# Experts' second product: one weight load for both parts of the activations, two halves of a bank added per expert

## The chip, the cores and the metric

The kernel runs on one core of a Trainium2 chip. The metric is the device time of one execution in microseconds, the median of several runs. Engines are named as the profile names them: PE is TensorE's matmul, PEld its weight load, DVE is VectorE, ACT ScalarE, POOL GpSimd, SP SyncE, whose queue issues most DMAs.

## What is computed

The reference is a chain of three parts, all in fp32 (q, k, v of 2 batches x 8 heads x 768 x 64; 1536 tokens of 512 features; 8 experts):

```python
state = gamma * state + k_t (x) v_t;  y_t = scale * q_t @ state    # linear attention, per head
e = argmax(x @ w_gate);  disp[e, slot] = x                         # dispatch, 8 experts
h = np.maximum(np.einsum('ecd,edf->ecf', disp, w1), 0.0)           # 512 -> 1024
y = np.einsum('ecf,efd->ecd', h, w2)                               # 1024 -> 512
out[i] = gate_w[i] * y[expert_idx[i], pos[i]]
h = x @ w_in;  g = h / (1 + exp(-h));  out = g @ w_out             # 512 -> 2048 -> 512
```

The change touches the second product of the experts, `y`.

## The kernel before

**Precision.** PE multiplies in a format (`F32R`) with fewer bits than fp32. So every operand is kept as two tiles, a high part (the value rounded to that format) and a low part (the value minus the high part), and every product is three matmuls into one sum: high x high, high x low, low x high.

**The order of the work.** Attention with gate and routing fills the first 75 us. Then the eight experts follow, each with at most 216 tokens (`SL`) in columns. An expert has eight weight units of 128 x 1024 (512 KB each): four of the first product, `stage_a(e, fu)` (lines 847 to 867), and four of the second, `stage_b(e, fu)` (869 to 879). Each unit holds 8 blocks of 128 x 128 and takes 24 matmuls. After that `finish(e)` (881 to 888) moves the result out of PSUM, and at the end come 12 steps of the dense FFN over quarters `q` of its hidden layer and groups `g` of 512 tokens (`s1`, `s2`, lines 940 to 998).

**The order is written out by hand.** The pool runs in manual schedule: each engine executes its instructions in the order of the program. The loop at lines 1002 to 1025 is: gather the next expert's rows, four `stage_a`, four `stage_b` (after the second of them the transposes of the next expert's rows, `xprep`, lines 813 to 818 and 557 to 565), then `finish(e)`. For the last expert `finish(7)` comes after the first FFN step (1042).

**Feed.** `advance(u)` (823 to 835) stands at the head of each unit. It issues the split of unit `u + 3`: ScalarE writes the high part (line 164), VectorE the low part (168), and the low part is issued one piece late, so that `advance(u)` issues the high part of unit `u + 3` and the low part of unit `u + 2`. It also issues the DMAs of later units, whose buffers come free with that low part, and every sixth unit from unit 9 on it puts in one piece of the FFN's weights (`ffn_piece`, lines 172 to 205: four VectorE, three ScalarE and two GpSimd instructions). In experts 1 and 2 VectorE also computes the token masks (898 to 918), a part after each second `stage_b`.

**PSUM.** From the experts on all tiles come from one pool of eight banks of 512 fp32 columns (807 to 811). An expert takes four banks for `h`, two for `y` and two for the transposes.

`stage_a` ends with the Relu of `h`: high part by ScalarE (863), low part by VectorE (864), into two tiles `hhi` and `hlo`. `stage_b` calls `three` (839 to 845) for each block: 256 blocks in all, of 8 experts x 4 units x 2 (`f`) x 4 (`d`), and each call loads weights three times, twice the same ones. Two of the four output blocks `d` share a bank of `y`. `finish` then takes, per bank, one ScalarE copy of 432 columns into `x2hi` and one VectorE subtraction into `x2lo`, at a column offset held in a register.

Of the kernel before, what the change touches and what calls it, by code (L numbers as in the profile page):

```python
# [8 lines left out]
F32 = mybir.dt.float32  # L9
F32R = mybir.dt.float32r  # L10
# [5 lines left out]
ALU = mybir.AluOpType  # L16
# [6 lines left out]
E = 8  # L23
F1 = 1024
F2 = 2048
P = 128
# [3 lines left out]
KD = DM // P  # L30
# [10 lines left out]
GT = NTOK // NG  # L41
# [13 lines left out]
def slots(cap):  # L55

    cap = max(0, min(cap, NTOK))
    sl = min(SLOTS, max(1, -(-cap // P)) * P)
    return cap, -(-sl // P), sl, -(-max(0, cap - sl) // P)
# [33 lines left out]
def moe_chain_kernel(ctx: ExitStack, tc: tile.TileContext, cap: int, a, out: bass.AP):  # L93
    nc = tc.nc
    ctx.enter_context(tc.manual_schedule())

    cap, nmain, SL, nover = slots(cap)
# [3 lines left out]
    SP = nmain * P  # L101
# [452 lines left out]
    moe = moe_stack.enter_context(tc.tile_pool(name="moe", side="right", bufs=1, reuse_waits="tile"))  # L554
# [100 lines left out]
    x2hi = ffn.tile([P, KD, NTOK + SP], F32R, name="x2hi")  # L655
    x2lo = ffn.tile([P, KD, NTOK + SP], F32R, name="x2lo")
# [3 lines left out]
    def fetch(e):  # L660
        xrows[e] = [gather_rows(rows, e, j, "xr", toki) for j in range(nmain)]
# [14 lines left out]
    with tc.If(over > capm, label="over"):  # L676
        with tc.tile_pool(name="gen", side="right", bufs=1) as gen, tc.tile_pool(name="gps", side="right", bufs=2, space=PSUM) as gps:
# [12 lines left out]
                out=god[:, :E], in0=god[:, :E], scalar1=gov[:, E : E + 1], scalar2=float(-cap), op0=ALU.add, op1=ALU.add  # L690
# [17 lines left out]
            if nover > 0:  # L708
# [3 lines left out]
                for j in range(nover):  # L712
                    nc.vector.scalar_tensor_tensor(
                        out=gstf[:, j], in0=gov[:, :E], scalar=float(j * P), in1=gov[:, 1:], op0=ALU.add, op1=ALU.min
# [11 lines left out]
                    out=slot, in0=ecol, scalar1=float(nover * P), scalar2=float(-capm), op0=ALU.mult, op1=ALU.add  # L726
# [3 lines left out]
                    out=block, in0=slot, scalar1=0.5 - P / 2, scalar2=ROUND, op0=ALU.add, op1=ALU.add  # L730
# [7 lines left out]
                    out=gohb, in0=cst[:, C_W : C_W + E * nover].unsqueeze(1).to_broadcast([P, NT, E * nover]),  # L738
                    in1=block.unsqueeze(2).to_broadcast([P, NT, E * nover]), op=ALU.is_equal,
                )  # L740
                nc.vector.tensor_tensor(
                    out=gohb, in0=gohb, in1=tokv.unsqueeze(2).to_broadcast([P, NT, E * nover]), op=ALU.mult
# [3 lines left out]
                    out=gohp, in0=iota_p.unsqueeze(1).to_broadcast([P, NT, P]),  # L746
                    in1=slot.unsqueeze(2).to_broadcast([P, NT, P]), op=ALU.is_equal,
# [10 lines left out]
                with tc.For_i(0, E, 1) as e:  # L758
                    now = gen.tile([P, 2, nover], I32, name="now")
                    nc.vector.tensor_copy(  # L760
                        out=now.unsqueeze(1), in_=gall[:, bass.ds(e, 1)]
                    )
                    for j in range(nover):
# [9 lines left out]
                        for r in range(8):  # L773
# [3 lines left out]
                            if r < 4:  # L777
                                gwv = gw.rearrange("p (d f m) -> p d f m", d=KD, f=2)
                                for f in range(2):
                                    hp = gps.tile([P, P], F32, tag="hp", name=f"hp{j}_{r}_{f}")  # L780
                                    for d in range(KD):
                                        nc.tensor.matmul(
                                            hp, lhsT=gwv[:, d, f], rhs=gxt[:, d], start=d == 0, stop=d == KD - 1
                                        )
                                    nc.scalar.activation(gh[:, 2 * r + f], hp, AF.Relu)
                            else:
                                gwv = gw.rearrange("p (f d m) -> p f d m", f=2, d=KD)
                                for f in range(2):
                                    ff = 2 * (r - 4) + f
                                    for d in range(KD):  # L790
                                        nc.tensor.matmul(
                                            yp[:, d], lhsT=gwv[:, f, d], rhs=gh[:, ff],
                                            start=ff == 0 and d == 0, stop=ff == 7, skip_group_check=True,
                                        )

                        win = bass.ds(r0, P)
                        nc.scalar.copy(out=x2hi[:, :, win], in_=yp)
                        nc.vector.tensor_tensor(
                            out=x2lo[:, :, win], in0=yp, in1=x2hi[:, :, win].bitcast(F32), op=ALU.subtract
# [10 lines left out]
    def bank(name):  # L810
        return ps.tile([P, 512], F32, tag="ps", name=name)
# [25 lines left out]
    htiles = {}  # L837

    def three(out_ap, l, r, first, last):

        lh, ll = l
        rh, rl = r
        nc.tensor.matmul(out_ap, lhsT=lh, rhs=rh, start=first, stop=False, skip_group_check=True)  # L843
        nc.tensor.matmul(out_ap, lhsT=lh, rhs=rl, start=False, stop=False, skip_group_check=True)  # L844
        nc.tensor.matmul(out_ap, lhsT=ll, rhs=rh, start=False, stop=last, skip_group_check=True)  # L845

    def stage_a(e, fu):
        u = 8 * e + fu
        advance(u)
        whi, wlo = [t.rearrange("p (d f m) -> p d f m", d=KD, f=2) for t in unit_tiles.pop(u)]  # L850
        xhi, xlo = xts[e]
        skip = {"skip_group_check": True}
        hb = bank(f"h{e}_{fu}").rearrange("p (f t) -> p f t", f=2)[:, :, :SL]
        for f in range(2):
            for d in range(KD):
                nc.tensor.matmul(hb[:, f], lhsT=whi[:, d, f], rhs=xhi[:, d], start=f == 0 and d == 0, stop=False, **skip)  # L856
                nc.tensor.matmul(hb[:, f], lhsT=wlo[:, d, f], rhs=xhi[:, d], start=False, stop=False, **skip)  # L857
        for f in range(2):
            for d in range(KD):
                nc.tensor.matmul(hb[:, f], lhsT=whi[:, d, f], rhs=xlo[:, d], start=False, stop=d == KD - 1, **skip)  # L860
        hhi = moe.tile([P, 2, SP], F32R, tag=f"hhi{fu}", name=f"hhi{e}_{fu}")[:, :, :SL]
        hlo = moe.tile([P, 2, SP], F32R, tag=f"hlo{fu}", name=f"hlo{e}_{fu}")[:, :, :SL]
        nc.scalar.activation(hhi, hb, AF.Relu)
        nc.vector.scalar_tensor_tensor(
            out=hlo, in0=hb, scalar=0.0, in1=hhi.bitcast(F32), op0=ALU.max, op1=ALU.subtract
        )
        htiles[fu] = (hhi, hlo)

    def stage_b(e, fu, yb):
        u = 8 * e + 4 + fu  # L870
        advance(u)
        whi, wlo = [t.rearrange("p (f d m) -> p f d m", f=2, d=KD) for t in unit_tiles.pop(u)]
        hhi, hlo = htiles[fu]
        for f in range(2):
            for d in range(KD):
                three(
                    yb[d // 2][:, d % 2], (whi[:, f, d], wlo[:, f, d]), (hhi[:, f], hlo[:, f]),
                    fu == 0 and f == 0 and d % 2 == 0, fu == 3 and f == 1,
                )

    def finish(e, yb):
        win = bass.ds(offr[e], SL)
        for b in range(2):
            ds2 = slice(2 * b, 2 * b + 2)
            nc.scalar.copy(out=x2hi[:, ds2, win], in_=yb[b])
            nc.vector.tensor_tensor(
                out=x2lo[:, ds2, win], in0=yb[b], in1=x2hi[:, ds2, win].bitcast(F32), op=ALU.subtract
            )


# [111 lines left out]
    for e in range(E):  # L1002
        if e + 1 < E:
            fetch(e + 1)
        for fu in range(4):
            stage_a(e, fu)
            if e == 0 and fu == 1:
                places = Places(const, "moe", False, edge)
                nc.vector.tensor_copy(out=offi, in_=places.start)
        if e == 0:  # L1010
            offr = [place_reg(offi[0:1, j : j + 1], max(0, NTOK - SL * (E - j)), NTOK) for j in range(E)]
        if e == 1:
            chores = token_masks(places)
        if e == 3:
            run(chores)
            token_table()
        yb = [bank(f"y{e}_{j}").rearrange("p (d t) -> p d t", d=2)[:, :, :SL] for j in range(2)]
        for fu in range(4):
            stage_b(e, fu, yb)
            if fu % 2 == 0:  # L1020
                next(chores, None)
            if fu == 1 and e + 1 < E:
                xprep(e + 1)
        if e + 1 < E:
            finish(e, yb)
# [4 lines left out]
    f2 = ctx.enter_context(tc.tile_pool(name="f2", bufs=1, reuse_waits="tile"))  # L1030
# [79 lines left out]
```

## Time and profile before

| | us |
|---|---|
| median of 3 runs | 525.29 (524.22 to 527.42) |
| the profiled execution | 521.98 |
| its span, first to last instruction | 520.2 |
| PE busy | 506.1 (97%) |
| VectorE busy | 319.9 (61%) |
| ScalarE busy | 243.7 (47%) |
| GpSimd busy | 152.6 (29%) |

The span runs from the first to the last instruction; the execution's time holds 1.8 us more. Busy times are of one profiled execution. A matmul's recorded duration holds its latency: a new one starts long before the recorded end of the last, so PE's rhythm is read from the starts. Times in rows are in microseconds from the start of the span, unless marked ns.

### The profile page before, as it was taken

How to read it: one execution, taken by the hardware profiler on the slowest of the kernel's cores; microseconds unless marked ns; L12 is line 12 of the kernel's file. 1: busy time of each engine (PE TensorE's matmuls, PEld its weight loads, DVE VectorE, ACT ScalarE, POOL GpSimd, SP SyncE). 2: the span in 40 equal slices, each digit the busy share in tenths (PEclk: the TensorE clock that was granted, in tenths of full speed). 3: DMA queues.
4: the chain of work that ended last, by engine and by line, in shares of the span. 5: the costliest groups of instructions: out<-in, count | busy, mean ns of one | idle time of the engine just before them, and what ended most of it. 6: DMA issues, size and time to landing. Idle time of an engine off the chain costs nothing.

```text
span 520.2 us, 9255 instructions
## 1 busy us (share of the span) xinstructions
PE 506.1 (97%) x3590; PEld 454.1 (87%) x3590; DVE 319.9 (61%) x663; ACT 243.7 (47%) x404; POOL 152.6 (29%) x144
## 2 busy tenths in 40 slices
PE   7999699999999999999999999999999999999995
PEld 5989689999999999999988888888888888888885
DVE  2667756788987887686176756457466574232441
ACT  2345535566665566555255655554254542212110
POOL 2545530105313243021015333251132511000315
PEclk8999999999999999999999999999999999999998
DMA  8999845877686667862013222131121200000203
GB/s 283 320 333 315 330 129 199 306 259 252 231 286 215 238 238 247 260 225 83 1 40 121 83 81 82 40 122 40 42 81 42 82 1 0 0 1 0 82 20 141
DMA packets 27151, 76.11 MB, mean 146 GB/s; under 512 B 3553, under 2 KB 6497, under 8 KB 27106
## 3 DMA queue, kind: packets, MB, share of 16 engines
q1 hardware_dynamic: 24416, 67.53, 38.4%
q0 software_dynamic: 2256, 7.34, 3.9%
q8 instruction: 28, 0.46, 0.3%
q10 hardware_dynamic: 434, 0.64, 0.3%
q14 instruction: 17, 0.14, 0.1%
HBM read 69.20 MB, written 6.29 MB: 145 GB/s over the span
## 4 chain that ended last, share of the span: by engine, by line
PE 74%; issue 14%; DMA 5%; POOL 3%; DVE 2%; ACT 0%; POOLq 0%; SPq 0%; DVEq 0%; ACTq 0%
PE s L843 11%; PE s L844 11%; PE s L845 11%; PE h L856 6%; PE h L857 6%; PE y L843 6%; PE y L845 5%; PE y L844 5%; PE h L860 5%; DMA q<-q 4%; PE A L335 2%; POOL out L981 2%; PE y L368 1%; PE g L401 1%; DMA gq<-gq 1%
## 5 line engine op out<-in xcount | busy, mean ns | idle before, releaser
L199 POOL TENSOR_TENSOR w<-w,ex 128x512 f32<-128x512 f32 x32 | 41.4, 1293 | 223.9 <-DVE ex L196 212.7
L952 DVE TENSOR_TENSOR gv<-s,gv 128x512 f32<-128x512 f32 x48 | 33.2, 692 | 86.9 <-ACT gv L951 86.8
L168 DVE TENSOR_TENSOR lo<-raw,hi 128x1024 fp32r<-128x1024 f32 x62 | 82.0, 1336 | 3.2 <-issue 2.3
L843 PE MATMUL s<-x2hi,hi 128*128 128x512 f32 x192 | 74.7, 389 | 0.0
L845 PE MATMUL s<-x2hi,lo 128*128 128x512 f32 x192 | 74.7, 389 | 0.0
L844 PE MATMUL s<-x2lo,hi 128*128 128x512 f32 x192 | 74.7, 389 | 0.0
L951 ACT ACTIVATE gv<-s 128x512 f32<-128x512 f32 x48 | 28.8, 599 | 97.7 <-PE s L845 97.7
L843 PE MATMUL y<-hhi,hi 128*128 128x216 f32 x256 | 70.8, 277 | 0.0
L845 PE MATMUL y<-hhi,lo 128*128 128x216 f32 x256 | 70.2, 274 | 0.0
L844 PE MATMUL y<-hlo,hi 128*128 128x216 f32 x256 | 70.2, 274 | 0.0
L843 PE MATMUL s<-hi,ghi 128*128 128x512 f32 x176 | 68.5, 389 | 0.0
L844 PE MATMUL s<-lo,ghi 128*128 128x512 f32 x176 | 68.5, 389 | 0.0
L845 PE MATMUL s<-hi,glo 128*128 128x512 f32 x176 | 68.5, 389 | 0.0
L164 ACT CAST hi<-raw 128x1024 fp32r<-128x1024 f32 x64 | 65.6, 1048 | 4.5 <-issue 2.3
L856 PE MATMUL h<-xthi,hi 128*128 128x216 f32 x256 | 58.9, 274 | 0.3 <-ACT xthi L564 0.3
L857 PE MATMUL h<-xthi,lo 128*128 128x216 f32 x256 | 58.8, 274 | 0.0
L954 DVE TENSOR_TENSOR glo<-gv,ghi 128x512 fp32r<-128x512 f32 x48 | 36.3, 757 | 32.9 <-ACT ghi L953 32.9
L203 POOL TENSOR_TENSOR lo<-w,hi 128x512 fp32r<-128x512 f32 x32 | 47.4, 1482 | 22.4 <-ACT hi L202 22.4
L856 PEld LDWEIGHTS h<-xthi,hi 128*128 128x128 f32 x256 | 49.1, 192 | 0.4 <-ACT xthi L564 0.4
L845 PEld LDWEIGHTS y<-hhi,lo 128*128 128x128 f32 x256 | 49.2, 192 | 0.0
L844 PEld LDWEIGHTS y<-hlo,hi 128*128 128x128 f32 x256 | 49.1, 192 | 0.0
L857 PEld LDWEIGHTS h<-xthi,lo 128*128 128x128 f32 x256 | 49.1, 192 | 0.0
(140 smaller groups left out, 931.2 us busy)
## 6 DMA issues: line engine op xcount, KB each, us to landing
raw<-w SPq DMA_DIRECT2D x64, 512.0 KB, 4.4
raw<-w_in SPq DMA_DIRECT2D x16, 512.0 KB, 3.5
raw<-w_out SPq DMA_DIRECT2D x16, 512.0 KB, 3.3
vk<-vk SPq DMA_DIRECT2D x11, 512.0 KB, 6.6
q<-q SPq DMA_DIRECT2D x12, 256.0 KB, 5.6
xtok<-xr SPq DMA_DIRECT2D x12, 256.0 KB, 4.3
kt<-kt SPq DMA_DIRECT2D x11, 256.0 KB, 5.3
gq<-gq SPq DMA_DIRECT2D x10, 128.0 KB, 6.0
```

Of the source, the lines that this page charges most:

```text
L164: nc.scalar.copy(out=hi, in_=t)
L168: lo_eng.tensor_tensor(out=lo, in0=t, in1=hi.bitcast(F32), op=ALU.subtract)
L199: nc.gpsimd.tensor_tensor(out=w, in0=w, in1=ex.bitcast(F32), op=ALU.mult)
L203: nc.gpsimd.tensor_tensor(out=lo[:, sl], in0=w, in1=hi[:, sl].bitcast(F32), op=ALU.subtract)
L843: nc.tensor.matmul(out_ap, lhsT=lh, rhs=rh, start=first, stop=False, skip_group_check=True)
L844: nc.tensor.matmul(out_ap, lhsT=lh, rhs=rl, start=False, stop=False, skip_group_check=True)
L845: nc.tensor.matmul(out_ap, lhsT=ll, rhs=rh, start=False, stop=last, skip_group_check=True)
L856: nc.tensor.matmul(hb[:, f], lhsT=whi[:, d, f], rhs=xhi[:, d], start=f == 0 and d == 0, stop=False, **skip)
L857: nc.tensor.matmul(hb[:, f], lhsT=wlo[:, d, f], rhs=xhi[:, d], start=False, stop=False, **skip)
L951: nc.scalar.activation(gv, hb, AF.Sigmoid)
L952: nc.vector.tensor_tensor(out=gv, in0=hb, in1=gv, op=ALU.mult)
L954: nc.vector.tensor_tensor(out=glo, in0=gv, in1=ghi.bitcast(F32), op=ALU.subtract)
```

## The change

`hhi` and `hlo` become one tile `hh` with the two parts side by side. In `stage_b` the high part of the weights is loaded once per block, and one matmul passes both parts of the activations under it, 2 x 216 columns, into the two halves of a bank (columns 0 to 215 and 256 to 471). The low part of the weights then passes the high activations into the second half. Each output block `d` has its own bank, four per expert. `finish` copies the second half out (ScalarE), adds the first half to it (VectorE), casts the sum to the high part (ScalarE) and subtracts (VectorE), for each `d` by itself, over two small tiles `ys`; for the last expert these come from the FFN's pool, from the buffers of `gv`.

```diff
-        hhi = moe.tile([P, 2, SP], F32R, tag=f"hhi{fu}", name=f"hhi{e}_{fu}")[:, :, :SL]
-        hlo = moe.tile([P, 2, SP], F32R, tag=f"hlo{fu}", name=f"hlo{e}_{fu}")[:, :, :SL]
+        hh = moe.tile([P, 2, 2, SP], F32R, tag=f"hh{fu}", name=f"hh{e}_{fu}")[:, :, :, :SL]
+        hhi, hlo = hh[:, 0], hh[:, 1]
...
-        htiles[fu] = (hhi, hlo)
+        htiles[fu] = hh
...
-        hhi, hlo = htiles[fu]
+        hh = htiles[fu]
+        skip = {"skip_group_check": True}
         for f in range(2):
             for d in range(KD):
-                three(
-                    yb[d // 2][:, d % 2], (whi[:, f, d], wlo[:, f, d]), (hhi[:, f], hlo[:, f]),
-                    fu == 0 and f == 0 and d % 2 == 0, fu == 3 and f == 1,
+                nc.tensor.matmul(
+                    yb[d][:, :, :SL], lhsT=whi[:, f, d], rhs=hh[:, :, f], start=fu == 0 and f == 0, stop=False, **skip
+                )
+                nc.tensor.matmul(
+                    yb[d][:, 1, :SL], lhsT=wlo[:, f, d], rhs=hh[:, 0, f], start=False, stop=fu == 3 and f == 1, **skip
                 )
 
     def finish(e, yb):
         win = bass.ds(offr[e], SL)
-        for b in range(2):
-            ds2 = slice(2 * b, 2 * b + 2)
-            nc.scalar.copy(out=x2hi[:, ds2, win], in_=yb[b])
+        for d in range(KD):
+            if e < E - 1:
+                ys = moe.tile([P, SP], F32, tag="ys", name=f"ys{e}_{d}", bufs=2)[:, :SL]
+            else:
+                ys = f2.tile([P, GT], F32, tag="gv", name=f"ys{e}_{d}", bufs=2)[:, :SL]
+            nc.scalar.copy(out=ys, in_=yb[d][:, 1, :SL])
+            nc.vector.tensor_tensor(out=ys, in0=yb[d][:, 0, :SL], in1=ys, op=ALU.add)
+            nc.scalar.copy(out=x2hi[:, d, win], in_=ys)
             nc.vector.tensor_tensor(
-                out=x2lo[:, ds2, win], in0=yb[b], in1=x2hi[:, ds2, win].bitcast(F32), op=ALU.subtract
+                out=x2lo[:, d, win], in0=ys, in1=x2hi[:, d, win].bitcast(F32), op=ALU.subtract
             )
...
-        yb = [bank(f"y{e}_{j}").rearrange("p (d t) -> p d t", d=2)[:, :, :SL] for j in range(2)]
+        yb = [bank(f"y{e}_{d}").rearrange("p (k t) -> p k t", k=2) for d in range(KD)]
```

## Rows read from the trace of the kernel before

**Rows 1.** Table by stage, experts 1 to 7: busy time (and instructions) of each engine.

```profile
core 0: us, PE busy (x) PEld busy (x) DVE busy (x) ACT busy (x) POOL busy (x), PEclk, DMA share, GB/s
...
97.59:253.26 155.67, 155.67 (x1407) 155.65 (x1405) 120.72 (x154) 92.08 (x132) 39.99 (x26) 1.00 0.66 227
```

**Rows 2.** Timeline of PE, expert 0, first unit of stage_b: start, duration.

```profile
86.00 0.28 PE L843 MATMUL y<-hhi,hi 128*128 128x216 f32 x1
...
88.68 0.28 PE L843 MATMUL y<-hhi,hi 128*128 128x216 f32 x1
```

**Rows 3.** Timeline of PE, matmuls of 512 and of 256 columns in the FFN.

```profile
264.18 0.39 PE L843 MATMUL s<-x2hi,hi 128*128 128x512 f32 x1
264.41 0.39 PE L844 MATMUL s<-x2lo,hi 128*128 128x512 f32 x1
...
512.05 0.28 PE L843 MATMUL s_last<-hi,ghi 128*128 128x256 f32 x1
512.17 0.28 PE L844 MATMUL s_last<-lo,ghi 128*128 128x256 f32 x1
```

**Rows 4.** Groups by line and shape, 84 to 254 us: busy us, mean ns | idle before.

```profile
L564 ACT CAST xthi<-xp 128x512 fp32r<-128x512 f32 x7 | 4.1, 586 | 13.4 <-PE xp L817 13.4
L564 ACT CAST xthi<-xp 128x352 fp32r<-128x352 f32 x7 | 3.2, 460 | 0.0
...
L565 DVE TENSOR_TENSOR xtlo<-xp,xthi 128x512 fp32r<-128x512 f32 x7 | 4.8, 692 | 5.5 <-ACT xthi L564 5.4
...
L565 DVE TENSOR_TENSOR xtlo<-xp,xthi 128x352 fp32r<-128x352 f32 x7 | 3.6, 514 | 0.0
...
L202 ACT CAST hi<-w 128x512 fp32r<-128x512 f32 x8 | 4.9, 608 | 0.0
```

**Rows 5.** Timeline, end of expert 3: ScalarE, VectorE and PE's next stage_a.

```profile
164.43 0.52 ACT L885 CAST x2hi<-y 128x432 f32 x1 [2.27 <-PE y L845]
...
164.90 0.27 PE L856 MATMUL h<-xthi,hi 128*128 128x216 f32 x1
...
164.98 1.28 DVE L886 TENSOR_TENSOR x2lo<-y,x2hi 128x432 f32 x2 [1.66 <-ACT x2hi L885]
166.18 1.22 DVE L168 TENSOR_TENSOR lo<-raw,hi 128x1024 fp32r<-128x1024 f32 x1
```

**Rows 6.** Timeline, ends of experts 1, 2 and 4: finish and PE's next stage_a.

```profile
114.30 0.94 ACT L564 CAST xthi<-xp 128x512 fp32r<-128x512 f32 x2 [3.38 <-PE xp L817]
...
119.89 0.27 PE L856 MATMUL h<-xthi,hi 128*128 128x216 f32 x1
...
120.73 1.12 DVE L886 TENSOR_TENSOR x2lo<-y,x2hi 128x432 f32 x2
...
142.20 0.27 PE L856 MATMUL h<-xthi,hi 128*128 128x216 f32 x1
...
143.22 1.11 DVE L886 TENSOR_TENSOR x2lo<-y,x2hi 128x432 f32 x2
...
187.21 0.27 PE L856 MATMUL h<-xthi,hi 128*128 128x216 f32 x1
...
187.68 1.12 DVE L886 TENSOR_TENSOR x2lo<-y,x2hi 128x432 f32 x2
```

**Rows 7.** Timeline of VectorE in stage_a of experts 1 and 4, with an FFN piece.

```profile
103.44 0.43 DVE L188 TENSOR_SCALAR ex<-raw 128x512 int32<-128x512 int32 x1 [0.67 <-DMA raw<-w_in]
...
106.04 2.03 DVE L168 TENSOR_TENSOR lo<-raw,hi 128x1024 fp32r<-128x1024 f32 x1
...
172.68 2.00 DVE L168 TENSOR_TENSOR lo<-raw,hi 128x1024 fp32r<-128x1024 f32 x1
```

**Rows 8.** Timeline of PE, a gap near the start: [idle before, releaser].

```profile
7.88 1.42 PE L335 MATMUL A<-q,kt 64*128 64x128 f32 x12 [2.21 <-DMA q<-q]
```

**Rows 9.** Table by stage, right behind that gap; the 0.50 is PE's granted clock.

```profile
8.20:11.50 3.30, 3.30 (x34) 3.08 (x32) 1.29 (x2) 0.82 (x2) 1.04 (x1) 0.50 0.99 301
```

**Rows 10.** Timeline, second FFN step: VectorE in finish(7), PE's second output bank.

```profile
267.06 1.12 DVE L886 TENSOR_TENSOR x2lo<-y,x2hi 128x432 f32 x2
...
267.36 0.19 PEld L843 LDWEIGHTS s<-hi,ghi 128*128 128x128 f32 x1
```

## The prediction

> **What bounds the kernel now.** I read the page first, where PE is busy nearly throughout; it says where to look, not what a change is worth. The table by stage shows that: from 97.59 to 253.26 us, experts 1 to 7, PE is busy in all of the 155.67 us at granted clock 1.00, while VectorE has 120.72 us of work and ScalarE 92.08 [rows 1]. The list of waits has no PE wait in this stretch. So time is saved only by making PE's stream shorter, and any new PE idle time is lost in full; VectorE, with 78% of the stretch filled, is the engine that could cause it.
>
> PE's own rhythm I read from the timeline. A unit of stage_b, 24 matmuls of 216 columns, takes 88.68 - 86.00 = 2.68 us [rows 2], 0.1117 each; stage_a has the same step. At 512 columns the step is 0.227 and at 256 it is 0.120 [rows 3]. The difference, 0.107 for 256 columns, is 0.418 ns a column, so a step is 0.013 us + 0.418 ns x columns; 216 columns would take 0.103. That they take 0.112 I put down to the load of the next weights, which at this width is a little longer than the stream and sets the step.
>
> **The change part by part.** *Matmuls.* Per (f, d) before: three loads and three matmuls, 3 x 0.1117 = 0.335 us. After: a 432-column matmul, 0.013 + 0.180 = 0.193, under which the next load is wholly hidden, and a 216-column one, 0.112. Sum 0.305, 0.030 less, and there are 8 experts x 4 x 2 x 4 = 256 of them: -7.7 us (0.96 per expert). If loads could run further ahead, the pair would cost 0.193 + 0.103 = 0.296: -10.0. If each of the two 216-column runs of the new matmul paid a step of its own, 2 x 0.112, the pair would cost 0.336: no gain. No row shows a matmul whose columns lie in two runs; I take one stream, since the rows at 256 and 512 columns show one fixed part per instruction, and keep both ends.
>
> [...]
>
> *The sum in finish.* Before, per expert: two ScalarE copies and two VectorE subtractions of 432 columns. After: four times a chain of copy (ScalarE), add (VectorE), cast (ScalarE), subtraction (VectorE), each of 216 columns. No row has these sizes. From PSUM, ScalarE takes 586 ns for 512 columns and 460 for 352, VectorE 692 and 514 [rows 4]: 0.79 and 1.11 ns a column, hence 0.35 and 0.36 at 216. The cast reads SBUF: 608 ns at 512 [rows 4], less 296 columns at that slope, 0.37. Subtraction: taken like the add, 0.37. A handover costs 0.03 (164.43 + 0.52 to 164.98), and an engine starts its next instruction 0.08 before the former's recorded end (166.18 against 164.98 + 1.28) [rows 5]. VectorE must finish add, wait for the cast, then start the subtraction before the next add: 0.37 + 0.03 + 0.37 + 0.03 + 0.30 = 1.10 us per d. The last subtraction starts 3 x 1.10 + 0.80 = 4.10 us after the first add, the next VectorE instruction 0.30 later. The ends: half of the 432-column prices (0.26 and 0.30) give 0.86 us per d; the 352-column prices give 1.46.
>
> *Who stands behind it.* Both queues are in order. Behind finish(e) on VectorE stands the low part of the weights of the third unit of the next stage_a (feed runs three units ahead; the second half of a piece is issued one piece late). It takes 1.22 us [rows 5] and ends at first add + 4.10 + 0.30 + 1.22 = add + 5.62. PE wants it after two units, 2 x 2.68 + 0.01 = 5.37 us after the new expert's first matmul, which I call T. So PE waits (add - T) + 0.25 us. The same low part lets go of a raw buffer, so SP's DMA into it, and the weight DMAs queued behind, go out as much later; the feed takes them up several units on, and I add nothing for them.
>
> When does the first add start? PE finishes yb[0] three pairs earlier than the rest: T - 3 x 0.305 - 0.112, plus 0.31 from matmul start to the copy's start (164.43 now, where the first bank's last matmul starts at 164.90 - 7 x 0.1117), plus copy and handover: T - 0.35. Wait: -0.10, so none. This holds after experts 0, 3, 5, 6, where ScalarE idles until y is there and VectorE is free [rows 5]: four ends at nothing, with a tenth to spare.
>
> After experts 1, 2 and 4 VectorE is late already, with FFN pieces and, in 1 and 2, token masks; its first subtraction stands at T + 0.84 (120.73 against 119.89), T + 1.02 (143.22 against 142.20) and T + 0.47 (187.68 against 187.21) [rows 6]. The shorter stage_b makes this worse: in 1 and 4 that work starts with the x transposes in mid-stage (114.30 [rows 6]), after which PE has two units left, 0.50 us shorter now; in 2 VectorE is behind from the stage's start, 0.96 shorter. Adds at T + 1.34, T + 1.98, T + 0.97: PE waits 1.6, 2.2 and 1.2 us.
>
> Two more waits come in the first unit of the next stage_b where an FFN piece falls in stage_a (experts 1 and 4). In expert 4 the low part that it needs ends at 172.68 + 2.00 [rows 7] = T + 9.78 (T = 164.90), wanted at T + 4 x 2.68 + 0.01 = T + 10.73. ScalarE's first Relu copy stood after the first unit, at T + 2.9 (its last matmul starts at 2.57, and 0.31); now the last cast (to T + 3.73) and a weights cast of 1.05 stand ahead of it: T + 4.6, 1.7 later, and both engines work without a gap from there: T + 11.5, 0.8 us late. In expert 1 it ends at 106.04 + 2.03 = T + 10.48 (T = 97.59); VectorE had 0.67 us of idle time ahead of it, for a DMA that need not come later [rows 7], so it moves 1.0: 0.75 late. Sum of waits: 1.6 + 2.2 + 1.2 + 0.8 + 0.75 = 6.6 us.
>
> *Banks.* Four y banks per expert instead of two. That costs nothing if no tile of the next expert waits for them. The pool hands out the bank let go first in program order, not the next by number: in the FFN's second step the second output bank is written without a wait (weights at 267.36) while x2lo of the first y bank still runs (267.06 for two instructions) [rows 10], which a ring by number would not allow. So y of one expert takes banks freed by the last finish, an expert ago, and the first FFN banks are those of h. Nothing is added; by a ring, PE would wait for finish(7) some 3.4 us. finish(7) delays one Sigmoid by 4 us; its output is used a whole step later. ys takes 2 KB per partition.
>
> *Sum.* -7.7 + 6.6 = -1.1 us. The profiled execution took 521.98 (span 520.2 and 1.8 around it), which becomes 520.9. The median of the runs shown is 525.29, 3.3 above it; put on the median: 524.2.
>
> **The rivals.** *Faster: the waits don't come.* If the chain costs 0.86 us per d, the last subtraction starts 1.0 us earlier: waits of 0.6, 1.2 and 0.2, none else; -5.7, or -8 with the shorter pair: 517 to 519.6. For it: the new operations are small, and VectorE has 22% idle time. Against: the durations at 352, 432 and 512 columns lie on one line with a fixed part.
>
> *Slower: the chain between ScalarE and VectorE in finish is longer than I price it.* At 1.46 per d the last subtraction starts 1.3 us later; then also the four free ends wait 1.2 each, the three late ones 2.9, 3.5 and 2.5, and some 1.5 remains for the stage_b units: 15 against 7.7, +7.5, 532.8. It turns into a loss from 1.15 us per d on, 0.05 above mine. Against: it needs 352-column prices for 216 columns.
>
> *Two runs cost two steps.* No gain; stage_b is as long as before, so the late ends shrink by 0.5, 1.0 and 0.5: waits 4.6, time 529.9. [...]
>
> *The clock falls in a wait.* A gap of 2.21 us ended at 7.88 [rows 8], and from 8.20 to 11.50 the granted clock was 0.50 [rows 9]: 3.4 us at half speed, 1.7 lost. Only the wait of 2.2 us comes near that gap: 525.9.
>
> **How the numbers follow.** Forecast 0.50; waits don't come 0.25; longer chain 0.12; two runs 0.08; clock 0.05. A difference under 1%, 5.25 us, is about what cannot be told from none here. Faster by more than that is the first rival: 0.25. Slower by more is the longer chain: 0.12. The rest, 0.63, lies within. The forecast's own range is 521 to 527; the range of 8 in 10 takes in most of both outer cases: 518.5 to 530.
>
> **What would show it.** 256 matmuls of 128x432 at steps of 0.193 and 256 of 0.112 show the first step right; 0.22 shows two runs. PE idle time, none before in experts 1 to 7, should stand at the third unit's low weights after experts 1, 2 and 4 (released by VectorE's L168 line), 1 to 2 us each, and at the first stage_b unit of experts 1 and 4. The four instructions of finish should repeat every 1.1 us. I am wrong if PE shows no waits there, or waits elsewhere (y banks, DMA of weights), or if the new matmul's step is not 0.193.

## The result, and the profile after

The changed kernel took 531.47 us (median of 15 runs, 527.45 to 536.03), the kernel before, timed with it, 525.5 (15 runs, 522.88 to 530.98). The ratio is 1.0103, 95% interval 1.0079 to 1.0128: slower by 4.2 to 6.7 us. It leaves out the slow execution of 536.03, 1.6% above the fastest, and so is not the quotient of the two medians. The forecast was 524.2, and the measured time lies 1.5 us above the upper end of the range.

The profiled execution took 529.81 us (span 528.0), 7.8 more than that of before. Of these, 2.5 us stand ahead of the experts: their first matmul starts at 77.66 us instead of 75.19, and in the executions of all kernels below, whose attention part is the same, that start lies anywhere between 75 and 82; another 0.5 us stands behind the last matmul. What the change touches is compared by the **experts' stretch**, from that matmul to the FFN's first: 178.07 us before, 182.87 after, +4.80. From there to the last matmul both took 261.19 us. On the medians the change costs 6.0 us; the 1.2 us beyond the 4.8 of this pair of executions are not explained by any run.

The page of the changed kernel, its second line, and of its costliest groups some of finish and stage_b, from 84 to 261 us (busy us, mean ns of one | idle time of the engine before them and its releaser):

```profile
PE 504.9 (96%) x3334; PEld 449.7 (85%) x3334; DVE 340.3 (64%) x711; ACT 254.3 (48%) x452; POOL 150.7 (29%) x144
...
L879 PE MATMUL y<-hh,hi 128*128 128x432 f32 x256 | 80.3, 373 | 0.0
L882 PE MATMUL y<-hh,lo 128*128 128x216 f32 x256 | 67.1, 262 | 1.1 <-DVE lo L168 1.1
...
L896 DVE TENSOR_TENSOR x2lo<-ys,x2hi 128x216 f32 x28 | 12.4, 442 | 12.4 <-ACT x2hi L895 11.9 <-DMA raw<-w 0.5
L894 DVE TENSOR_TENSOR ys<-y,ys 128x216 f32<-128x216 f32 x28 | 10.5, 376 | 2.0 <-ACT ys L893 2.0
L895 ACT CAST x2hi<-ys 128x216 f32 x28 | 10.5, 373 | 18.1 <-DVE ys L894 13.8 <-DVE lo L168 2.7 <-DVE x2lo L896 1.6
```

PE's share of the span hardly moved, and says nothing of why the time did. The groups of finish hold the first hint: 11.9 us in which VectorE waited for ScalarE's cast, and 13.8 in which ScalarE waited for VectorE's add. The list of PE's waits, 75 to 260 us (us in total, times, longest), shows who pays for it:

```profile
PE h L857 <- DVE lo L168: 5.9, 3, 2.1
PE y L882 <- DVE lo L168: 1.1, 2, 0.6
PE h L856 <- ACT xthi L564: 0.3, 1, 0.3
```

Before, this list had no PE wait in experts 1 to 7. Now there are five, each for the low part of the weights. The table by stage has the rest: experts 1 to 7, which answers to [rows 1], then the stretches behind the first, the second and the third of the long waits:

```profile
core 0: us, PE busy (x) PEld busy (x) DVE busy (x) ACT busy (x) POOL busy (x), PEclk, DMA share, GB/s
99.17:260.53 161.36, 154.35 (x1183) 151.36 (x1181) 131.79 (x196) 101.77 (x173) 36.87 (x26) 0.98 0.66 220
130.40:133.70 3.30, 3.30 (x17) 3.30 (x17) 2.08 (x3) 1.05 (x2) 0.00 (x0) 0.50 0.83 258
155.60:158.90 3.30, 3.30 (x32) 3.30 (x31) 3.12 (x5) 2.51 (x5) 0.00 (x0) 1.00 0.84 254
202.00:205.40 3.40, 3.40 (x19) 3.40 (x18) 1.99 (x4) 1.38 (x3) 0.00 (x0) 0.50 0.85 269
```

The granted clock of experts 1 to 7 fell from 1.00 to 0.98. It was 0.50 for 3.4 us behind the first long wait and again behind the third; 17 matmuls stand in 3.30 us and 19 in 3.40, against 32 in 3.30 us at 1.00 behind the second wait, where there was no fall. At half speed each fall cost 3.4 / 2 = 1.7 us. The profiled execution is no exception in this: the mean granted clock of a whole execution was 0.984 in the change (median of its 15) and 0.991 in the kernel before (median of 37 executions timed beside the experiments); over 528 us this difference is 3.7 us.

PE's timeline, first the new pair in expert 0 (it answers to [rows 2]), then, for experts 2, 3 and 5, the first matmul of stage_a and the one that waited:

```profile
88.48 0.37 PE L879 MATMUL y<-hh,hi 128*128 128x432 f32 x1
88.68 0.26 PE L882 MATMUL y<-hh,lo 128*128 128x216 f32 x1
88.78 0.37 PE L879 MATMUL y<-hh,hi 128*128 128x432 f32 x1
...
121.51 0.27 PE L856 MATMUL h<-xthi,hi 128*128 128x216 f32 x1
...
126.87 0.27 PE L856 MATMUL h<-xthi,hi 128*128 128x216 f32 x1
129.23 0.37 PE L857 MATMUL h<-xthi,lo 128*128 128x216 f32 x1 [2.09 <-DVE lo L168]
...
146.90 0.27 PE L856 MATMUL h<-xthi,hi 128*128 128x216 f32 x1
...
154.55 0.37 PE L857 MATMUL h<-xthi,lo 128*128 128x216 f32 x1 [2.02 <-DVE lo L168]
...
193.23 0.27 PE L856 MATMUL h<-xthi,hi 128*128 128x216 f32 x1
...
200.65 0.37 PE L857 MATMUL h<-xthi,lo 128*128 128x216 f32 x1 [1.78 <-DVE lo L168]
```

The pair steps by 88.78 - 88.48 = 0.30. Over whole units the mean is 0.306, and two stage_b units together are 0.445 us shorter than before: 16 x 0.445 = 7.1 us saved over the 32 units. The idle time in brackets counts from the recorded end of the matmul before, 0.27 after its start; without a wait the next starts 0.11 after it. What PE really lost is the excess of the step: 129.23 - 126.87 - 0.11 = 2.25, where 2.09 is listed. I call this **lateness**. The five come to 0.75 (stage_b of expert 1), 2.25, 2.18, 0.70 (stage_b of expert 4) and 1.94, in all 7.8 us.

So the stretch's +4.8 is -7.1 (matmuls) + 7.8 (five waits) + 3.4 (two falls of the clock), with 0.7 left for small gaps.

What finish does on VectorE at the end of expert 1, which answers to [rows 6]:

```profile
122.73 0.38 DVE L894 TENSOR_TENSOR ys<-y,ys 128x216 f32<-128x216 f32 x1
123.54 0.87 DVE L896 TENSOR_TENSOR x2lo<-ys,x2hi 128x216 f32 x1 [0.44 <-ACT x2hi L895]
124.34 0.37 DVE L894 TENSOR_TENSOR ys<-y,ys 128x216 f32<-128x216 f32 x1
125.15 0.66 DVE L896 TENSOR_TENSOR x2lo<-ys,x2hi 128x216 f32 x1 [0.44 <-ACT x2hi L895]
125.73 0.37 DVE L894 TENSOR_TENSOR ys<-y,ys 128x216 f32<-128x216 f32 x1
126.54 0.38 DVE L896 TENSOR_TENSOR x2lo<-ys,x2hi 128x216 f32 x1 [0.44 <-ACT x2hi L895]
126.84 0.38 DVE L894 TENSOR_TENSOR ys<-y,ys 128x216 f32<-128x216 f32 x1
127.66 0.39 DVE L896 TENSOR_TENSOR x2lo<-ys,x2hi 128x216 f32 x1 [0.44 <-ACT x2hi L895]
127.96 1.22 DVE L168 TENSOR_TENSOR lo<-raw,hi 128x1024 fp32r<-128x1024 f32 x1
```

The undisturbed cycle is 126.84 - 125.73 = 1.11 us, of which VectorE stands idle for 0.44. The low part that PE wants comes last, ends at 129.18, and PE starts at 129.23. The first two subtractions took 0.87 and 0.66 us. GpSimd's timeline has something beside both, a piece of the FFN's weights:

```profile
122.89 1.28 POOL L199 TENSOR_TENSOR w<-w,ex 128x512 f32<-128x512 f32 x1 [13.12 <-DVE ex L196]
124.13 1.44 POOL L203 TENSOR_TENSOR lo<-w,hi 128x512 fp32r<-128x512 f32 x1
```

### The profile page after: what moved, and what is told of

Read it like the earlier page. It is cut to its first block, busy times and chain, and to the rows that moved or that the text cites. A ratio compares the mean times of both kernels' runs of the same rounds, so it can differ in the third digit from the quotient of the medians.

```text
span 528.0 us, 8848 instructions
## 1 busy us (share of the span) xinstructions
PE 504.9 (96%) x3334; PEld 449.7 (85%) x3334; DVE 340.3 (64%) x711; ACT 254.3 (48%) x452; POOL 150.7 (29%) x144
## 4 chain that ended last, share of the span: by engine, by line
PE 60%; issue 16%; DVE 13%; DMA 4%; ACT 3%; POOL 3%; SPq 1%; ACTq 0%; POOLq 0%; DVEq 0%
PE s L843 11%; PE s L845 11%; PE s L844 11%; PE y L879 6%; DVE lo L168 4%; PE h L857 3%; PE h L860 3%; PE h L856 3%; PE y L882 3%; PE A L335 2%; PE y L368 2%; PE g L401 2%; POOL out L991 1%; DVE x2lo L896 1%; PE y L362 1%
## 5 line engine op out<-in xcount | busy, mean ns | idle before, releaser
L879 PE MATMUL y<-hh,hi 128*128 128x432 f32 x256 | 80.3, 373 | 0.0
L882 PE MATMUL y<-hh,lo 128*128 128x216 f32 x256 | 67.1, 262 | 1.1 <-DVE lo L168 1.1
L857 PE MATMUL h<-xthi,lo 128*128 128x216 f32 x256 | 60.8, 281 | 5.9 <-DVE lo L168 5.9
L964 DVE TENSOR_TENSOR glo<-gv,ghi 128x512 fp32r<-128x512 f32 x48 | 41.2, 859 | 33.0 <-ACT ghi L963 33.0
L856 PE MATMUL h<-xthi,hi 128*128 128x216 f32 x256 | 60.6, 279 | 0.3 <-ACT xthi L564 0.3
L857 PEld LDWEIGHTS h<-xthi,lo 128*128 128x128 f32 x256 | 50.2, 196 | 6.6 <-DVE lo L168 6.4
L203 POOL TENSOR_TENSOR lo<-w,hi 128x512 fp32r<-128x512 f32 x32 | 45.7, 1429 | 23.3 <-ACT hi L202 23.3
L882 PEld LDWEIGHTS y<-hh,lo 128*128 128x128 f32 x256 | 48.9, 191 | 1.7 <-DVE lo L168 1.7
L879 PEld LDWEIGHTS y<-hh,hi 128*128 128x128 f32 x256 | 48.1, 188 | 1.9
L963 ACT CAST ghi<-gv 128x512 fp32r<-128x512 f32 x48 | 29.8, 621 | 36.8 <-DVE gv L962 36.8
```

Of the source, the lines that this page charges most:

```text
L203: nc.gpsimd.tensor_tensor(out=lo[:, sl], in0=w, in1=hi[:, sl].bitcast(F32), op=ALU.subtract)
L879: nc.tensor.matmul(yb[d][:, :, :SL], lhsT=whi[:, f, d], rhs=hh[:, :, f], start=fu == 0 and f == 0, stop=False, **skip)
L882: nc.tensor.matmul(yb[d][:, 1, :SL], lhsT=wlo[:, f, d], rhs=hh[:, 0, f], start=False, stop=fu == 3 and f == 1, **skip)
L964: nc.vector.tensor_tensor(out=glo, in0=gv, in1=ghi.bitcast(F32), op=ALU.subtract)
```

## The experiments

Each was timed against the kernel before on the same chip (ratios with 95% intervals); two were executed only once. The stretch, the lateness and the falls are of one profiled execution each. The edits are to the changed kernel, except in the control.

| run | median us | ratio | experts' stretch | lateness in sum | falls of the clock in it |
|---|---|---|---|---|---|
| before | 525.5 | 1 | 178.07 | 0 | 0 |
| the change | 531.47 | 1.0103 (1.0079 to 1.0128) | 182.87 | 7.8 | 2 |
| matmuls alone | 519.42 | 0.9872 (0.9825 to 0.9919) | 171.65 | 0.6 | 0 |
| sum alone | 532.40 | 1.0153 (1.0114 to 1.0191) | 186.02 | 5.9 | 1 |
| sum by kind | 521.42 | 0.9919 (0.9885 to 0.9953) | 173.66 | 1.9 | 0 |
| low weights last | 520.71 | 0.9925 (0.9897 to 0.9954) | 173.78 | 2.8 | 0 |
| both of these | 518.33 | 0.9844 (0.9815 to 0.9872) | 171.16 | 0 | 0 |
| control: before, low weights last | 525.34 | 0.9997 (0.9971 to 1.0022) | 178.07 | 0 | 0 |
| waits filled | 527.49 | 1.0008 (0.9982 to 1.0033) | 179.82 | (filled) | 0 |
| one run of columns (executed once) | 531.37 | | 182.74 | 7.7 | 2 |
| low weights before finish (executed once) | 529.10 | | 180.72 | 8.5 | 0 |

**The matmuls alone.** The new matmuls into four banks, with the old finish on two of them; the sum of the halves and the other two banks are left out of the result:

```diff
     def finish(e, yb):
         win = bass.ds(offr[e], SL)
-        for d in range(KD):
...
+        for b in range(2):
+            ds2 = slice(2 * b, 2 * b + 2)
+            nc.scalar.copy(out=x2hi[:, ds2, win], in_=yb[b][:, :, :SL])
             nc.vector.tensor_tensor(
-                out=x2lo[:, d, win], in0=ys, in1=x2hi[:, d, win].bitcast(F32), op=ALU.subtract
+                out=x2lo[:, ds2, win], in0=yb[b][:, :, :SL], in1=x2hi[:, ds2, win].bitcast(F32), op=ALU.subtract
             )
```

> The changed kernel's matmuls and four banks, but finish with the two copies and two subtractions of 432 columns of the kernel before, on the first two of the four banks; the sum of the halves and the other two banks are left out of the result. Theory (the matmul pair is worth 28 ns per block, and all that is lost comes from the new finish on ScalarE and VectorE): no PE wait in experts 1 to 7, the clock stays at full speed there, 256 x 28 ns = 7.1 us less than before: about 518.4, ratio 0.986. Rival (the loss sits in the new matmuls or the banks, for instance in the clock under longer matmuls): 523 or more, ratio above 0.995.

The stretch was 171.65 us, 6.4 below before: the 7.1 less one wait of 0.6 in stage_b of expert 1. The saving on PE is there in full, and all of the loss but this wait comes only with the new finish. No wait was expected; this one has another cause. ScalarE's timeline there has the first instruction of an FFN piece, which waited for the DMA of its own input:

```profile
110.19 0.67 ACT L187 ACTIVATE lf<-raw 128x512 f32<-128x512 uint32 x1 [2.40 <-DMA raw<-w_in]
```

**The sum alone.** Three matmuls with three loads again, the new finish:

```diff
-                nc.tensor.matmul(
-                    yb[d][:, :, :SL], lhsT=whi[:, f, d], rhs=hh[:, :, f], start=fu == 0 and f == 0, stop=False, **skip
-                )
+                first = fu == 0 and f == 0
+                nc.tensor.matmul(yb[d][:, 0, :SL], lhsT=whi[:, f, d], rhs=hh[:, 0, f], start=first, stop=False, **skip)
+                nc.tensor.matmul(yb[d][:, 1, :SL], lhsT=whi[:, f, d], rhs=hh[:, 1, f], start=False, stop=False, **skip)
```

> The new finish and the four banks, but three matmuls of 216 columns with three weight loads per block, as before. Theory: the waits for the third unit's low weights after experts 1, 2 and 4 are there, shorter than in the changed kernel by the 0.5, 0.9 and 0.5 us that stage_b is longer: about 1.8, 1.3 and 1.5, the two of 0.85 in the first units of stage_b stay, in all some 6.3 us, and up to two falls of the clock at 1.7 each: 532 to 535, ratio 1.012 to 1.018. Rival (a stage_b of the old length hides the sum): 527 or less, ratio below 1.003.

PE's waits in this run, and the table by stage behind the first long one:

```profile
PE h L857 <- DVE lo L168: 4.1, 3, 1.7
PE y L882 <- DVE lo L168: 0.9, 2, 0.5
```

```profile
130.50:133.80 3.30, 3.30 (x18) 3.30 (x17) 2.57 (x3) 1.40 (x3) 0.00 (x0) 0.50 0.75 245
```

The same five waits stand in the same places with the old, longer stage_b: lateness 0.61, 1.81, 1.31, 0.63 and 1.51. So the new finish makes them without the new matmuls; only the one in stage_b of expert 1 comes with the matmuls alone as well. In the change the three long ones are 0.44, 0.87 and 0.43 longer: that is what the shorter stage_b adds, where the prediction had 0.50, 0.96 and 0.50. One wait here, listed at 1.65 us, was followed by a fall of the clock.

**The sum by kind.** The same sixteen instructions, ordered four copies, four adds, four casts, four subtractions, over four `ys` tiles (`hh` is packed to make room for them; the last expert stays as it was):

```diff
+        if e < E - 1:
+            yss = [moe.tile([P, SP], F32, tag="ys", name=f"ys{e}_{d}", bufs=4)[:, :SL] for d in range(KD)]
+            for d in range(KD):
+                nc.scalar.copy(out=yss[d], in_=yb[d][:, 1, :SL])
+            for d in range(KD):
+                nc.vector.tensor_tensor(out=yss[d], in0=yb[d][:, 0, :SL], in1=yss[d], op=ALU.add)
+            for d in range(KD):
+                nc.scalar.copy(out=x2hi[:, d, win], in_=yss[d])
+            for d in range(KD):
+                nc.vector.tensor_tensor(
+                    out=x2lo[:, d, win], in0=yss[d], in1=x2hi[:, d, win].bitcast(F32), op=ALU.subtract
+                )
+            return
```

> The changed kernel with finish in another order: four copies, four adds, four casts, four subtractions, over four small tiles in place of two (the tile hh is packed more tightly to make room). Same instructions, but ScalarE and VectorE no longer wait for each other inside each d. Theory (the wait is the chain of 1.1 us per d): VectorE is through with finish about 2 us earlier, the waits of 2.3, 2.2 and 2.0 fall to 0.3, 0.2 and 0, those in stage_b to 0, and the clock no longer falls: about 518 to 520, ratio 0.987 to 0.990. Rival (it is VectorE's work in finish as such, eight instructions instead of two, that PE waits for): 529 or more, ratio above 1.006.

VectorE's timeline at the end of expert 1, and PE's waits:

```profile
124.29 1.24 DVE L893 TENSOR_TENSOR ys<-y,ys 128x216 f32<-128x216 f32 x4
125.45 2.55 DVE L897 TENSOR_TENSOR x2lo<-ys,x2hi 128x216 f32 x4
127.93 1.21 DVE L168 TENSOR_TENSOR lo<-raw,hi 128x1024 fp32r<-128x1024 f32 x1
```

```profile
PE y L882 <- DVE lo L168: 0.8, 1, 0.8
PE h L857 <- DVE lo L168: 0.6, 2, 0.5
```

From the first add to the start of the low part it is 127.93 - 124.29 = 3.64 us, against 127.96 - 122.73 = 5.23 in the change: VectorE no longer stands idle for the cast. Lateness fell from 7.8 to 1.9, no fall of the clock was left, and the stretch came to 173.66 us. The alternation of the two engines, not the number of instructions, is what cost. The time, 521.42, lies above the 518 to 520 expected. One part was missed: the wait in stage_b of expert 1, expected to go, stayed at 0.93. As with the matmuls alone, ScalarE's timeline has an FFN instruction ahead of the weights' high part that waited for the DMA of its own input, which the order of finish does not touch:

```profile
107.67 0.69 ACT L187 ACTIVATE lf<-raw 128x512 f32<-128x512 uint32 x1 [2.73 <-DMA raw<-w_in]
```

**The low weights last.** PE passes all matmuls under the high weights of a unit first, and those under the low weights at its end, in stage_a (shown) and in stage_b:

```diff
                 nc.tensor.matmul(hb[:, f], lhsT=whi[:, d, f], rhs=xhi[:, d], start=f == 0 and d == 0, stop=False, **skip)
-                nc.tensor.matmul(hb[:, f], lhsT=wlo[:, d, f], rhs=xhi[:, d], start=False, stop=False, **skip)
...
+        for f in range(2):
+            for d in range(KD):
+                nc.tensor.matmul(hb[:, f], lhsT=wlo[:, d, f], rhs=xhi[:, d], start=False, stop=d == KD - 1, **skip)
```

> The changed kernel with PE's matmuls of a unit in another order: all that use the high part of the weights first, those with the low part last, in stage_a (16 before 8) and in stage_b (8 before 8). ScalarE and VectorE are untouched. Theory (PE waits for the low part of one unit, and no more is late behind it): the low part is wanted 1.8 us later in stage_a and 1.7 later in stage_b, waits fall from 2.3, 2.2, 2.0, 0.9 and 0.8 to 0.5, 0.4, 0.2, 0 and 0, no fall of the clock: about 519.5, ratio 0.988. Rival (VectorE or ScalarE is behind for good, and PE waits for it elsewhere, at hh or the next low part): 527 or more, ratio above 1.003.

PE's waits, and its timeline in the first stage_b unit of expert 0:

```profile
PE h L862 <- DVE lo L168: 2.3, 3, 1.2
```

```profile
89.14 1.73 PE L879 MATMUL y<-hh,hi 128*128 128x432 f32 x8
90.71 1.04 PE L884 MATMUL y<-hh,lo 128*128 128x216 f32 x8
91.59 0.76 PE L879 MATMUL y<-hh,hi 128*128 128x432 f32 x3
```

PE wants the low part 15 matmuls, 1.7 us, later in the unit, and lateness fell to 1.37, 0.93 and 0.49, more than was expected (0.5, 0.4, 0.2): PE waits less ahead of each of them too (in stage_b of experts 1 and 4 not at all, in expert 2 0.9 us less), so it also reaches them earlier. Time 520.71, where 519.5 was expected; no fall of the clock in the experts. The rows give a second thing: in a row, the 432-column matmuls step by (90.71 - 89.14) / 8 = 0.196 and the 216-column ones by (91.59 - 90.71) / 8 = 0.110, close to the 0.193 and 0.112 of the prediction. In turn they show as 0.208 and 0.098 (medians of the change), with the same sum.

**Both, and the control.** Sum by kind and low weights last together; and the kernel before with the low weights last in stage_a, to see whether that order is worth something by itself.

> Finish by kind and low weights last together. Theory: no PE wait in experts 1 to 7, no fall of the clock there; experts in 178.1 - 7.1 = 171.0 us, median about 518.4, ratio 0.986, below either alone (173.7 and 173.8 us in their profiles). Rival (what is left in those two is not waits for low weights): 520.5 or more, ratio above 0.990.

> The kernel before with the stage_a order of low weights last, as a control. Theory: it has no wait there, so nothing changes: experts in 178.1 us, ratio 0.998 to 1.002. Rival (the order by itself makes PE's stream shorter): 523 or less, ratio below 0.996.

The table by stage over the experts of the first, and the whole list of PE's waits in them:

```profile
79.64:250.80 171.16, 171.16 (x1349) 169.05 (x1349) 145.22 (x225) 110.98 (x188) 43.54 (x30) 1.00 0.70 231
```

```profile
PE h L856 <- ACT xthi L564: 0.3, 1, 0.3
```

PE is busy in all of the 171.16 us, 6.9 less than before: nearly the whole 7.1. At 518.33 us this version beats both kernels. The control's 0.9997 shows that the order of PE in stage_a alone gains nothing where nothing is late.

**The waits filled.** Nine more matmuls of 2 x 216 columns, into a bank that nobody reads, ahead of the late low part in experts 2, 3 and 5, so that PE has work where it waited:

```diff
+                if f == 0 and d == 0 and fu == 2 and e in (2, 3, 5):
+                    wb = bank(f"fill{e}").rearrange("p (f t) -> p f t", f=2)[:, :, :SL]
+                    for _ in range(9):
+                        nc.tensor.matmul(wb, lhsT=whi[:, d, f], rhs=xhi[:, :2], start=True, stop=True, **skip)
```

> The changed kernel with nine matmuls of 2 x 216 columns more (1.87 us) into a bank that nobody reads, just ahead of the first use of the low weights in the third unit of experts 2, 3 and 5, where PE waited 2.1, 2.0 and 1.8 us. The waits stay as time, but PE has work in them. Theory (a wait of some 2 us makes the granted clock fall afterwards, at 1.7 us each): no 0.50 in experts 1 to 7, experts in 179.5 us instead of 182.9 in the profile, median about 528, ratio 1.005 to 1.007. Rival (the clock falls there for another reason, such as the stream of longer matmuls, or the fall costs nothing): the falls stay, or the median stays at 531 or more, ratio above 1.009.

```profile
80.26:260.08 179.82, 177.83 (x1375) 173.96 (x1376) 147.16 (x225) 112.69 (x188) 42.49 (x30) 1.00 0.66 220
```

This row of the table by stage, the experts of this run, has the granted clock at 1.00 again, and the stretch is 3.05 us shorter than the change's 182.87, though in each expert PE reaches the late low part no earlier. By expert, from its first matmul to the next one's: experts 2 and 5, where the clock had fallen, went from 25.39 to 23.77 us and from 25.08 to 23.46; expert 3, with as long a wait but no fall, took 24.08 in both. So the clock's share of the loss, worked out as 3.4, is shown, at 1.62 us a fall: work that computes nothing gives it back. Over whole executions the mean granted clock was back at 0.9915 (median of 10). The ratio, 1.0008, came out below the 1.005 to 1.007 expected; the change was not timed beside this run, so the clock's share rests on the stretch and not on the medians.

**One run of columns.** `hh` laid out so that the 432-column matmul reads and writes one run instead of two:

```diff
-        hh = moe.tile([P, 2, 2, SP], F32R, tag=f"hh{fu}", name=f"hh{e}_{fu}")[:, :, :, :SL]
-        hhi, hlo = hh[:, 0], hh[:, 1]
+        hh = moe.tile([P, 2, 2, SL], F32R, tag=f"hh{fu}", name=f"hh{e}_{fu}")
+        hhi, hlo = hh[:, :, 0], hh[:, :, 1]
...
-        yb = [bank(f"y{e}_{d}").rearrange("p (k t) -> p k t", k=2) for d in range(KD)]
+        yb = [bank(f"y{e}_{d}")[:, : 2 * SL].rearrange("p (k t) -> p k t", k=2) for d in range(KD)]
```

> The changed kernel with both parts of the activations next to each other, so that the new matmul reads and writes one run of 432 columns in place of two of 216. It took 0.208 us, not 0.193. Theory A (the second run pays a fixed part of its own, about 14 ns): the step falls to 0.193 to 0.195 and the pair of matmuls from 0.306 to 0.292. Theory B (the pair is set by its two loads and streams together, not by the runs): the pair stays at 0.304 to 0.308, however it is shared out.

PE's timeline, first stage_b unit of expert 0:

```profile
90.12 0.37 PE L879 MATMUL y<-hh,hi 128*128 128x432 f32 x1
...
90.73 0.37 PE L879 MATMUL y<-hh,hi 128*128 128x432 f32 x1
```

Two pairs take 90.73 - 90.12 = 0.61, as with two runs, and the stretch is 182.74 against 182.87. So in this pair the two runs of 216 columns cost nothing: it takes 0.305 with one run and 0.306 with two.

**The low weights before finish.** The third unit's low part is issued on VectorE ahead of finish, not behind it:

```diff
         if e + 1 < E:
+            moe_feed.flush()
             finish(e, yb)
```

> The changed kernel with the low part of the third unit's weights issued on VectorE ahead of finish instead of behind it, after each expert. Theory (what stands behind finish on the two queues is late, whichever piece it is): the waits of 2.1, 2.0 and 1.8 us in the third unit of experts 2, 3 and 5 go, but where VectorE was late already (after experts 1, 2 and 4) finish itself starts 1.1 us later, and the next low part, behind finish, a cast on ScalarE and the first Relu, comes some 1.7, 2.3 and 1.3 us after the fourth unit wants it: waits of that size in the fourth unit, experts in 180 to 183 us. Rival (only the one piece behind finish matters, all else has slack): no wait in the third or fourth unit, experts in 171 to 173 us.

VectorE's timeline after finish(1), and PE's waits:

```profile
131.55 0.61 DVE L864 SCALAR_TENSOR_TENSOR hh<-h,hh 128x432 fp32r<-128x432 f32 x1 [0.99 <-ACT hh L863]
132.07 1.22 DVE L168 TENSOR_TENSOR lo<-raw,hi 128x1024 fp32r<-128x1024 f32 x1
```

```profile
PE h L857 <- DVE lo L168: 5.2, 3, 1.8
PE y L882 <- DVE lo L168: 2.3, 2, 1.5
```

The three long waits did not go; they moved one unit on, to the fourth, with lateness 2.09, 2.09 and 1.72, since there the low part now waits behind finish and behind ScalarE's Relu (0.99 us idle). The lateness in sum is even larger, 8.5. The stretch was still 2.15 us shorter than the change's, because no fall of the clock came, after listed waits of 1.83, 1.84 and 1.56.

## Why the prediction was wrong, and where it was right

**Matmuls: right.** The pair was forecast at 0.305 and took 0.306; -7.1 us measured against -7.7. The difference is small: 0.028 per pair instead of 0.030. That the load of the next weights sets the 0.112, and is hidden under 432 columns, was inferred from the steps at 256 and 512 columns; no run changes the load alone. The prediction named a step other than 0.193 as a sign against it: in turn the new matmul steps by 0.208, but what it has more the 216-column one has less (0.098 for 0.112), so the sum holds and the shares do not. The bank argument [rows 10] held too: no wait for a `y` bank in any run.

**Places of the waits: right.** Third unit's low weights after experts 1, 2 and 4, first stage_b unit of experts 1 and 4, next to nothing elsewhere. The undisturbed chain was forecast at 1.10 us per `d` and 4.10 from the first add to the last subtraction; after expert 2 it took 4.16. The two stage_b waits were forecast at 0.75 and 0.8 and came to 0.75 and 0.70. The first of these has a second cause that the prediction had ruled out ("a DMA that need not come later"): without the new chain, in the run with the matmuls alone, PE still waited 0.6 us there, behind that DMA. In the change VectorE worked without a gap ahead of it, as forecast.

**Failed: "Subtraction: taken like the add, 0.37."** It took 0.38 alone, but 0.87 and 0.66 after expert 1 and 0.94 and 0.66 after expert 4. The chain there was 127.66 - 122.73 = 4.93 and 4.99 us instead of 4.10. With the first adds nearly where they were forecast (T + 1.22, 1.92 and 0.86; forecast T + 1.34, 1.98 and 0.97), the waits came to 2.25, 2.18 and 1.94 instead of 1.6, 2.2 and 1.2: the first and the last are too small by just this. The long ones are those that lie beside GpSimd's FFN piece. I had priced the add and the subtraction alike, but the add reads one input from PSUM and the subtraction now both from SBUF. Before, the subtraction read PSUM, and two of them took 1.12 beside GpSimd's piece and 1.11 without [rows 6], the piece standing in the timeline of before at

```profile
120.83 1.30 POOL L199 TENSOR_TENSOR w<-w,ex 128x512 f32<-128x512 f32 x1 [13.85 <-DVE ex L196]
```

So the trace of the change ties the slow subtractions to GpSimd in all four cases: the first two after experts 1 and 4 are slow (0.66 to 0.94) and all others take 0.38 to 0.39, also those beside GpSimd's row gathers. No run took GpSimd's piece away, and none shows by what mechanism the subtraction is slower beside it. The price stood in the trace of before, overlooked: the low part of the weights, which has both inputs in SBUF too, took 1.21 to 1.23 us alone from 75 to 260 us and 1.28 to 2.31 in all 13 cases in which one of the piece's two GpSimd instructions ran as it began. The 2.03 and 2.00 of [rows 7] are two of them; beside the first stood

```profile
105.69 1.29 POOL L199 TENSOR_TENSOR w<-w,ex 128x512 f32<-128x512 f32 x1 [11.15 <-DMA raw<-w_in]
```

**Failed: "The clock falls in a wait."** This rival had 5%, and only for the one wait of 2.2 us, at 1.7. The cost of one fall was right (1.62 by the run with the waits filled); it came twice, 3.4 us in sum, behind listed waits of 2.09 and 1.78. This is the larger of the two errors, and the run with the waits filled shows it. I had compared the wait with the single gap between matmuls in the trace of before that a fall followed (2.21 us [rows 8, 9]), and taken the shorter ones as safe, for which no row spoke.

With both, the sum of the prediction reads -7.1 + 7.8 + 3.4 = +4.1 where it had -7.7 + 6.6 = -1.1; with the small gaps it is the measured +4.8.

**The rivals.** "The waits don't come", at 25%, is refuted by the trace, and "two runs cost two steps" by the run with one run of columns (0.305 a pair, 0.306 with two). "The chain is longer than I price it" has the right sign, but not at its place: the cycle is 1.11, not 1.46, the free ends after experts 0, 3, 5 and 6 stayed free, and the added length (4.93 and 4.99 instead of 4.10) stood beside GpSimd's pieces. What the list lacked was the two of them together: waits a little longer, and the clock after more than one.

**Open.** What decides whether the clock falls. Falls followed listed waits of 2.09 and 1.78 (the change), 2.10 and 1.79 (one run of columns) and 1.65 (sum alone). None followed 2.02 (the change), 2.01 (one run), or 1.83, 1.84 and 1.56 (low weights before finish). The length of the wait alone does not decide.

## What to carry to other kernels

Where the bound engine is full, a saving on it is worth what the engines that feed it let through (here 7.1 us were saved and 7.8 lost in waits): ask what stands behind each added instruction in its queue, and by when the bound engine wants that. A chain that goes to and fro between two engines is better issued by kind than item by item, and an operand that comes late is better used last; here the two edits turn +1.0% into -1.6%. An idle time of PE may cost twice, once as the wait and once more in the clock behind it, as two of the five did here: 2.25 and 1.94 us late, and 1.7 more for each.

## What the runs showed of the hardware that was not expected

- Within a stretch in which PE was otherwise busy throughout, the granted clock went to 0.50 for 3.4 us behind waits listed at 1.65 us (sum alone), 1.78 and 2.09 (the change), and each fall cost 1.6 to 1.7 us (1.62 by the run with the waits filled, 3.4 / 2 by the clock). Work without use in the waits kept it at 1.00 there.
- A VectorE subtraction of 128x216 with both inputs in SBUF took 0.66 to 0.94 us beside GpSimd's 128x512 products and subtractions of the FFN pieces, 0.38 to 0.39 without and beside its row gathers; issued four in a row (sum by kind), the four took 2.55 us after expert 1 and 2.62 after expert 4. The add beside it, with one input in PSUM, stayed at 0.37 to 0.38.
- A 432-column matmul in two runs steps like one in one run: with a 216-column one behind it 0.306 and 0.305. In turn with a 216-column one the steps are 0.208 and 0.098, in a row 0.196 and 0.110: the sum per pair is the same.
- The idle time listed before a matmul is 0.16 us less than what PE lost: 2.09 for 2.25, 2.02 for 2.18 and 1.78 for 1.94 in the change.
